# Low parts of weights and h in the first tile of the first MoE: from GpSimd to VectorE

## The chip, the cores and the metric

The kernel runs on one core of a Trainium2 chip. A core has TensorE (PE in the profile, its weight loads PEld), VectorE (DVE), ScalarE (ACT), GpSimd (POOL) and SyncE (SP, which here only issues transfers). The metric is the device time of one execution in microseconds.

## The reference, cut to what matters

Attention over chunks of 32 tokens gives x (3072 tokens, 512 wide). Two feed-forward blocks follow. The change lies in the first of them:

```python
def _moe_ref(x, w_gate, w_val, w_out, rms_g):      # w_gate, w_val 512 x 1536, w_out 1536 x 512
    rms = np.sqrt(np.mean(x * x, axis=-1, keepdims=True) + 1e-06)
    xn = x / rms * rms_g
    g = xn @ w_gate
    silu = g * (1.0 / (1.0 + np.exp(-g)))
    val = xn @ w_val
    return (silu * val @ w_out).astype(np.float32)
```

## The kernel before, in words

Every product of the feed-forward blocks is made of three matmuls: a float32 operand is split into a rounded **high part** and a **low part** (operand minus high part), and mm3 (L534 to L536) adds high x high, high x low and low x high. `split` makes the two parts: ScalarE writes the high part (L106), then an engine that the caller names writes the low part by one subtraction over 128 x 512 (L107).

The first MoE takes the tokens in tiles of 512; t counts the tiles, and this case is about t = 0. In a tile, f runs over 12 blocks of 128 hidden columns. For each f TensorE computes the gate product in ps_g0 and the value product in ps_g1 (12 matmuls each); ScalarE applies Silu (L811), VectorE multiplies (L816) to s, which is the h of this block, and `split_h` splits s into hh and hl. The output product of the block before (`out1`, 12 matmuls, which need hh and hl) follows on TensorE.

The weights come as 36 units in the order gate, value, out of f = 0, of f = 1 and so on. They arrive as float64 words, and in tile t = 0 one unit is converted at each of the 36 slots (three in each f):

- `load_w` transfers a unit into one of three buffers named w64 (L114, on SP's queue).
- `conv_c` scales one word half into a buffer tu (ScalarE, L122); there are three such buffers.
- `conv_d` joins the bits on VectorE, with three instructions in a chain (L132, L135, L138). When the last of them is done, the w64 buffer is free for the load of the unit three places on.
- `conv_g` splits tu into the high and low part in the resident tile `wall` (L106, L107). Then tu is free for the unit three places on.

The four units of the first slots are converted in a part written out by hand before the first tile (the string ORDER), and 32 are left for t = 0. Between the slots of t = 0 stand the steps of attention for later tokens, on TensorE with one PSUM tile ps_a: s (scores, L391; then VectorE takes m, L404, and e, L407, and ScalarE the exponential, L416), a (transpose of e, L421; ScalarE copies it to aT, L427), v (product with v, L437; VectorE normalizes, L458 to L464), r (row scaling on VectorE, L502) and x (transpose, L512; ScalarE copies it to xn, L523). One pair of such steps takes six values of f:

```python
plan = {1: "s0", 3: "a0", 4: "v0", 7: "s1", 9: "a1", 10: "v1", 11: "r0", 14: "x0", 15: "x1"}
```

In t = 0 only the queues of TensorE and SP are in the order in which the code is written; a scheduler sets the order on VectorE, ScalarE and GpSimd from its own estimate of the work. From t = 1 on every queue is in written order. All queues are executed strictly in order. Exponential and Silu need different tables on ScalarE, so each exponential brings two rows ACT_TABLE_LOAD.

Of the kernel before, what the change touches and what calls it, by code (L numbers as in the profile page):

```python
# [8 lines left out]
F32 = mybir.dt.float32  # L9
# [29 lines left out]
def tile_stream_attention_moe_moe2(  # L39
# [10 lines left out]
    nc = tc.nc  # L50
# [54 lines left out]
    def split(hi, lo, src, eng_lo):  # L105
        nc.scalar.activation(hi, src, AF.Copy)  # L106
        eng_lo.tensor_tensor(out=lo, in0=src, in1=hi.bitcast(F32), op=ALU.subtract)  # L107
# [9 lines left out]
    def conv_c():  # L117


        dst, key, w64 = raw.pop(0)  # L120
        tu = tmp.tile([P, 512], U32, tag="tu", name="tu")
        nc.scalar.activation(tu.bitcast(F32), words(w64)[1].bitcast(F32), AF.Copy, scale=2.0 ** -112)  # L122
        absd.append((dst, key, w64, tu))
# [18 lines left out]
    def conv_d():  # L142
        dst, key, w64, tu = absd.pop(0)
        join(tu, w64)
        f32s.append((dst, key, tu))

    def conv_g():
        dst, key, tu = f32s.pop(0)
        w = wall[:, 3 * key[1] + "gvo".index(key[0])]
        split(w[:, 0], w[:, 1], tu.bitcast(F32), nc.gpsimd)  # L150
        dst[key] = (w[:, 0], w[:, 1])

    def conv_w():

        n = len(absd)
        if f32s:
            conv_g()
        if raw:
            conv_c()
        if n:  # L160
            conv_d()
# [165 lines left out]
    def split_x(src):  # L327
        for kk in range(KK):
            x_hi(src, kk, slice(0, TT))
            x_lo(src, kk, slice(0, TT), nc.vector)  # L330
# [196 lines left out]
    def load_x(t):  # L527
        xn_t[t] = xs.tile([P, KK, TT], F32, tag="xn", name="xn")
        nc.sync.dma_start(xn_t[t], x_d[t])
# [8 lines left out]
    def proj_in(ps, unit):  # L538
        wh, wl = unit
        for kk in range(KK):  # L540
            sl = slice(kk * P, (kk + 1) * P)
            mm3(ps, (wh[:, sl], wl[:, sl]), xhl[kk], kk == 0, kk == KK - 1)

    h_t = {}

    def split_h(key, h, eng_lo):
        hi = hp_.tile([P, TT], F32R, tag="hh", name="hh")
        lo = hp_.tile([P, TT], F32R, tag="hl", name="hl")
        split(hi, lo, h, eng_lo)
        h_t[key] = (hi, lo)  # L550

    def evacuate(dst):
# [6 lines left out]
    def out1(t, f):  # L559
        h = h_t.pop(f)  # L560
        wh, wl = w1[("o", f)]
        for m in range(KK):
            sl = slice(m * P, (m + 1) * P)
            mm3(ps_y[m], (wh[:, sl], wl[:, sl]), h, f == 0, f == F1 - 1)
        if f == F1 - 1:
            ys = xs.tile([P, KK, TT], F32, tag="xn", name="ys")
            evacuate(ys)
            nc.sync.dma_start(y_d[t], ys)
# [26 lines left out]
    for st in ORDER.split():  # L595
# [28 lines left out]
        elif c == "r":  # L624
            step_r(n // 2, (n % 2,))
        elif c == "p":
            part_p(n)
        elif c in "HL":
            kk, o = divmod(n, 2)
            part = slice(o * PT, o * PT + PT)  # L630
            if c == "H":
                x_hi(xn_t[0], kk, part)
            else:
                x_lo(xn_t[0], kk, part, nc.gpsimd if st in LO_ON_POOL else nc.vector)
        elif c == "G":
            cols = slice(n % 2 * PT, n % 2 * PT + PT)
            for x in x_t[n // 2]:
                nc.gpsimd.tensor_tensor(out=x[:, cols], in0=x[:, cols], in1=g_b[:, cols], op=ALU.mult)
        elif c == "R":
            pr, blk = divmod(n, 2)  # L640
            x = x_t[pr][blk]
            nc.scalar.activation(x, x, AF.Copy, scale=rs_t[pr][:, blk:blk + 1])
        elif c == "c":
            conv_c()
        elif c == "d":
            conv_d()
            load_w(units1, 1)
        elif c == "g":
            conv_g()
        else:  # L650
            fns[c](n)
            if c in "mAn":
                free.append(use.pop(({"m": "s", "A": "a", "n": "v"}[c], n)))
# [56 lines left out]
    def slot(t, s):  # L710
        att_slot(t, s)
        if t == 0:
            conv_w()
            load_w(units1, 1)
        else:
            if xq:
                xq.pop(0)()

            n = 36 * t - 36 + s
            conv_step(2 if n < 48 else 7 / 3 if n < 88 else 3)  # L720
# [16 lines left out]
    def load_y(*src):  # L737
        for o in range(2):
            nc.sync.dma_start(m2["y"][:, o], src[o])


    def load_wp(n):
        if n < F1 + NP2 * G2:
            src = w1p_d[n] if n < F1 else w2p_d[(n - F1) % G2]
            nc.sync.dma_start(wp[:, n % 2].bitcast(F32), src)
# [17 lines left out]
    def x_steps(e):  # L763
        y = m2["y"]
        B11, B21, B12, B22 = y[:, 0, 0:2], y[:, 0, 2:4], y[:, 1, 0:2], y[:, 1, 2:4]
        tt = nc.vector.tensor_tensor

        def hi(c, x):
            nc.scalar.activation(xb[:, 2 * c:2 * c + 2, 0], x, AF.Copy)

        def lo(c, x):
            tt(
                out=xb[:, 2 * c:2 * c + 2, 1],
                in0=x,
                in1=xb[:, 2 * c:2 * c + 2, 0].bitcast(F32),
                op=ALU.subtract,
            )


        yield lambda: tt(out=e, in0=B12, in1=B11, op=ALU.subtract)  # L780
        yield lambda: tt(out=B12, in0=B22, in1=B12, op=ALU.subtract)
        yield lambda: (hi(0, B11), hi(2, e))
        yield lambda: (lo(0, B11), hi(3, B12))
        yield lambda: (tt(out=B11, in0=B12, in1=B11, op=ALU.add), hi(1, B11))
        yield lambda: (lo(1, B11), hi(4, B21))
        yield lambda: (lo(2, e), hi(5, B22))
        yield lambda: lo(3, B12)
        yield lambda: lo(4, B21)
        yield lambda: (tt(out=B21, in0=B21, in1=B11, op=ALU.subtract), hi(6, B21))
        yield lambda: lo(5, B22)  # L790
        yield lambda: lo(6, B21)

    for t in range(NS):
        if t == 1:
            region.close()
            region.enter_context(tc.manual_schedule())
        for f in range(F1):
            if t == NS - 1 and f == 6:
                att_only.close()
                right = ctx.enter_context(tc.tile_pool(name="right", bufs=1, side="right", reuse_waits="tile"))  # L800
                m2["y"] = right.tile([P, 2, KK, TT], F32, name="y")
                load_y(x_d[NS], x_d[NS + 1])
            if t == NS - 1 and f == 7:
                xq.extend(x_steps(xs.tile([P, 2, TT], F32, tag="xn", name="e")))
            if 0 < t < NS - 1 and f == 9:
                load_x(t + 1)
            if t == NS - 1 and f == F1 - 1:
                load_wp(0)
            proj_in(ps_g[0], w1[("g", f)])
            s = sp.tile([P, TT], F32, tag="s", name="s")  # L810
            nc.scalar.activation(s, ps_g[0], AF.Silu)  # L811
            slot(t, 3 * f)
            proj_in(ps_g[1], w1[("v", f)])
            if f == F1 - 1 and t + 1 < NS:
                split_x(xn_t.pop(t + 1))
            nc.vector.tensor_tensor(out=s, in0=s, in1=ps_g[1], op=ALU.mult)  # L816
            split_h(f, s, nc.gpsimd if t == 0 else nc.vector)
            slot(t, 3 * f + 1)
            if pend is not None:
                out1(*pend)  # L820
            pend = (t, f)
            slot(t, 3 * f + 2)
# [298 lines left out]
```

## Time and profile before

| | us |
|---|---|
| median of 3 runs | 1215.93 (1214.59 to 1216.49) |
| the profiled execution | 1213.37 |
| its span (first to last instruction) | 1211.6 |
| busy: TensorE matmul | 1169.8 (97%) |
| busy: VectorE | 761.2 (63%) |
| busy: ScalarE | 496.8 (41%) |
| busy: GpSimd | 171.2 (14%) |

The profiled execution is 1.8 us longer than its span. The busy shares are means over stages that differ; the tile t = 0 lies between about 41 and 168 us of the span.

### The profile page before, as it was taken

The numbers are of one execution on the slowest core, as the hardware profiler recorded it, in microseconds if no ns is written. First come the engines' busy times: TensorE is split into PE (matmuls) and PEld (weight loads), VectorE is DVE, ScalarE is ACT, GpSimd is POOL, SyncE is SP. The second block draws the span as 40 slices with busy tenths as digits, with TensorE's granted clock in tenths as the row PEclk, the third lists the DMA queues.
The fourth block names the chain that finished last, engine by engine and source line by source line (L and its number), as shares of the span: only waits on it lengthen the run. The fifth ranks groups of instructions, "written<-read, shape, count | busy, mean of one in ns | idle before, by whom it ended". The sixth has DMA issues, their size and how long they took to land.

```text
span 1211.6 us, 19907 instructions
## 1 busy us (share of the span) xinstructions
PE 1169.8 (97%) x7993; PEld 940.8 (78%) x7993; DVE 761.2 (63%) x1256; ACT 496.8 (41%) x830; POOL 171.2 (14%) x219
## 2 busy tenths in 40 slices
PE   7888899999999999889999999999999999999998
PEld 4666677777777778668888788888888888888887
DVE  5898856656656665866767728666176664466620
ACT  4665655455544653433333414334043332233310
POOL 2655421121221212212101000000000000000000
PEclk8898999999999999989999999999999999999999
DMA  8555538887957666489787766756565656555354
GB/s 300 181 187 179 185 113 276 289 287 252 327 178 232 208 230 219 177 319 322 284 355 267 291 226 237 266 195 243 198 223 197 260 199 219 198 209 191 131 191 156
DMA packets 98061, 278.60 MB, mean 230 GB/s; under 512 B 10032, under 2 KB 22320, under 8 KB 91568
## 3 DMA queue, kind: packets, MB, share of 16 engines
q1 hardware_dynamic: 79408, 218.59, 51.5%
q0 software_dynamic: 15104, 52.44, 12.1%
q10 hardware_dynamic: 3456, 6.29, 1.4%
q8 instruction: 63, 1.03, 0.3%
q14 instruction: 30, 0.25, 0.1%
HBM read 209.13 MB, written 68.16 MB: 229 GB/s over the span
## 4 chain that ended last, share of the span: by engine, by line
PE 54%; DMA 2%; DVE 2%; ACT 0%; issue 0%; POOL 0%; SPq 0%; DVEq 0%; ACTq 0%
PE ps_y L975 7%; PE ps_y L974 7%; PE ps_y L973 7%; PE ps_b L836 5%; PE ps_b L837 5%; PE ps_b L838 5%; PE ps_g L836 4%; PE ps_g L838 4%; PE ps_g L837 4%; PE ps_y L535 2%; PE ps_y L536 2%; PE ps_y L534 2%; DMA w<-in_w_dram 1%; DMA wo<-w1o_d 1%; DMA y_d<-ys 1%
## 5 line engine op out<-in xcount | busy, mean ns | idle before, releaser
L534 PE MATMUL ps_g<-xh,wall 128*128 128x512 f32 x384 | 159.3, 415 | 3.3 <-ACT s L811 2.2
L536 PE MATMUL ps_g<-xh,wall 128*128 128x512 f32 x384 | 153.6, 400 | 0.0
L535 PE MATMUL ps_g<-xl,wall 128*128 128x512 f32 x384 | 153.4, 400 | 0.0
L973 PE MATMUL ps_y<-wo,wall 128*128 128x512 f32 x324 | 126.0, 389 | 0.0
L974 PE MATMUL ps_y<-wo,wall 128*128 128x512 f32 x324 | 126.0, 389 | 0.0
L975 PE MATMUL ps_y<-wo,wall 128*128 128x512 f32 x324 | 126.0, 389 | 0.0
L897 ACT ACTIVATE t<-t,half 128x512 f32<-128x512 f32 x96 | 69.0, 720 | 132.0 <-DVE t L896 132.0
L836 PE MATMUL ps_b<-wall 128*128 128x512 f32 x288 | 112.8, 392 | 0.2 <-DVE p L869 0.2
L837 PE MATMUL ps_b<-wall 128*128 128x512 f32 x288 | 112.5, 391 | 0.0
L838 PE MATMUL ps_b<-wall 128*128 128x512 f32 x288 | 112.4, 390 | 0.0
L534 PEld LDWEIGHTS ps_g<-xh,wall 128*128 128x128 f32 x384 | 73.6, 192 | 21.9 <-ACT s L811 3.1
L836 PE MATMUL ps_g<-wall 128*128 128x512 f32 x216 | 84.5, 391 | 3.5 <-ACT p L863 3.5
L911 DVE TENSOR_TENSOR t<-t,ps_g 128x512 f32<-128x512 f32 x24 | 16.5, 688 | 112.6 <-PE ps_g L838 107.7
L536 PEld LDWEIGHTS ps_g<-xh,wall 128*128 128x128 f32 x384 | 73.2, 191 | 17.8
L535 PEld LDWEIGHTS ps_g<-xl,wall 128*128 128x128 f32 x384 | 73.7, 192 | 15.4
L838 PE MATMUL ps_g<-wall 128*128 128x512 f32 x216 | 84.3, 390 | 0.0
L837 PE MATMUL ps_g<-wall 128*128 128x512 f32 x216 | 84.3, 390 | 0.0
L534 PE MATMUL ps_y<-hh,wall 128*128 128x512 f32 x192 | 78.7, 410 | 1.0 <-ACT hh L106 1.0
L535 PE MATMUL ps_y<-hl,wall 128*128 128x512 f32 x192 | 75.9, 396 | 0.2 <-DVE hl L107 0.2
L536 PE MATMUL ps_y<-hh,wall 128*128 128x512 f32 x192 | 76.0, 396 | 0.0
L974 PEld LDWEIGHTS ps_y<-wo,wall 128*128 128x128 f32 x324 | 60.8, 188 | 12.7
L973 PEld LDWEIGHTS ps_y<-wo,wall 128*128 128x128 f32 x324 | 60.8, 188 | 12.6
(155 smaller groups left out, 2304.5 us busy)
## 6 DMA issues: line engine op xcount, KB each, us to landing
wo<-w2o_d SPq DMA_DIRECT2D x100, 512.0 KB, 4.7
wall<-w2p_d SPq DMA_DIRECT2D x24, 1792.0 KB, 7.4
wall<-w1p_d SPq DMA_DIRECT2D x12, 1792.0 KB, 8.8
w<-in_w_dram SPq DMA_DIRECT2D x36, 512.0 KB, 4.1
w<-in_w_dram POOLq DMA_DIRECT2D x32, 512.0 KB, 5.6
k_in<-in_k_dram SPq DMA_DIRECT2D x48, 256.0 KB, 4.4
wo<-w1o_d SPq DMA_DIRECT2D x24, 512.0 KB, 7.4
v_in<-in_v_dram SPq DMA_DIRECT2D x40, 260.0 KB, 4.1
```

Source lines behind the costliest of these rows:

```text
L534: nc.tensor.matmul(ps, wh, xh, start=start, stop=False)
L535: nc.tensor.matmul(ps, wh, xl, start=False, stop=False)
L536: nc.tensor.matmul(ps, wl, xh, start=False, stop=stop)
L836: nc.tensor.matmul(bank, wh, xh, start=st, stop=False, skip_group_check=True)
L837: nc.tensor.matmul(bank, wh, xl, start=False, stop=False, skip_group_check=True)
L838: nc.tensor.matmul(bank, wl, xh, start=False, stop=kk == 1, skip_group_check=True)
L897: nc.scalar.activation(s, s, AF.Square, scale=0.5, bias=half)
L911: tt(out=u2, in0=a, in1=b2, op=ALU.add)
L973: nc.tensor.matmul(ps_y[m], hi[:, sl], wh, start=b == 0, stop=False)
L974: nc.tensor.matmul(ps_y[m], hi[:, sl], wl, start=False, stop=False)
L975: nc.tensor.matmul(ps_y[m], lo[:, sl], wh, start=False, stop=b == F2 - 1)
```

## The change

In t = 0 the low parts of the weights (`conv_g` out of `conv_w`) and of h (`split_h`) are subtracted by VectorE. The calls out of ORDER keep GpSimd, and from t = 1 on h was split on VectorE before too.

```diff
-    def conv_g():
+    def conv_g(eng_lo=nc.gpsimd):
         dst, key, tu = f32s.pop(0)
         w = wall[:, 3 * key[1] + "gvo".index(key[0])]
-        split(w[:, 0], w[:, 1], tu.bitcast(F32), nc.gpsimd)
+        split(w[:, 0], w[:, 1], tu.bitcast(F32), eng_lo)
         dst[key] = (w[:, 0], w[:, 1])
     def conv_w():
         n = len(absd)
         if f32s:
-            conv_g()
+            conv_g(nc.vector)
...
-    def split_h(key, h, eng_lo):
+    def split_h(key, h):
         hi = hp_.tile([P, TT], F32R, tag="hh", name="hh")
         lo = hp_.tile([P, TT], F32R, tag="hl", name="hl")
-        split(hi, lo, h, eng_lo)
+        split(hi, lo, h, nc.vector)
         h_t[key] = (hi, lo)
...
-            split_h(f, s, nc.gpsimd if t == 0 else nc.vector)
+            split_h(f, s)
```

The orders of TensorE and SP are the same before and after. GpSimd loses 44 rows of L107 (32 of weights, 12 of h), and VectorE has them more; the scheduler also sets the other rows of VectorE and ScalarE anew. A number behind tu names a unit: tu_923 and tu_944 are the ninth and tenth of all, tu_967, tu_1036, tu_1057 and tu_1086 the next four.

**First place: VectorE around the first scores of the tile** (m_1023 and e_1025, from the step s in f = 2; s_963 is the h of f = 2). Before:

```order
L138 SCALAR_TENSOR_TENSOR tu_967<-w64_853,tu_967 128x512
L132 TENSOR_SCALAR tu_1036<-tu_1036 128x512
L135 SCALAR_TENSOR_TENSOR tu_1036<-w64_928,tu_1036 128x512
L138 SCALAR_TENSOR_TENSOR tu_1036<-w64_928,tu_1036 128x512
L132 TENSOR_SCALAR tu_1057<-tu_1057 128x512
L135 SCALAR_TENSOR_TENSOR tu_1057<-w64_949,tu_1057 128x512
L816 TENSOR_TENSOR s_963<-s_963,ps_g1_104 128x512
L138 SCALAR_TENSOR_TENSOR tu_1057<-w64_949,tu_1057 128x512
L404 TENSOR_REDUCE m_1023<-ps_a_102 128x8
L132 TENSOR_SCALAR tu_1086<-tu_1086 128x512
L407 TENSOR_TENSOR e_1025<-ps_a_102,m_1023 128x2x4x64
```

After:

```order
L138 SCALAR_TENSOR_TENSOR tu_967<-w64_853,tu_967 128x512
L816 TENSOR_TENSOR s_963<-s_963,ps_g1_104 128x512
L132 TENSOR_SCALAR tu_1036<-tu_1036 128x512
L135 SCALAR_TENSOR_TENSOR tu_1036<-w64_928,tu_1036 128x512
L404 TENSOR_REDUCE m_1023<-ps_a_102 128x8
L107 TENSOR_TENSOR hl_988<-s_963,hh_987 128x512
L407 TENSOR_TENSOR e_1025<-ps_a_102,m_1023 128x2x4x64
L107 TENSOR_TENSOR wall_97<-tu_967,wall_97 128x512
L138 SCALAR_TENSOR_TENSOR tu_1036<-w64_928,tu_1036 128x512
```

Between L138 of tu_967 and e stood nine rows and stand five: the end of tu_1036, all of tu_1057 and the start of tu_1086 went behind e, and one low part came ahead of it.

**Second place: ScalarE around its first copy to xn** (L523, in f = 4, which the transpose of step x in f = 5 waits for). Before:

```order
L106 ACTIVATE wall_97<-tu_1207 128x512
L122 ACTIVATE tu_1233<-w64_1166 128x512
L811 ACTIVATE s_1203<-ps_g0_103 128x512
L122 ACTIVATE tu_1260<-w64_1189 128x512
L106 ACTIVATE wall_97<-tu_1233 128x512
L122 ACTIVATE tu_1288<-w64_1212 128x512
L106 ACTIVATE wall_97<-tu_1260 128x512
L106 ACTIVATE hh_1227<-s_1203 128x512
L122 ACTIVATE tu_1314<-w64_1238 128x512
L106 ACTIVATE wall_97<-tu_1288 128x512
L523 ACTIVATE xn_1252<-ps_a_102 128x4x128
```

After:

```order
L811 ACTIVATE s_1203<-ps_g0_103 128x512
L122 ACTIVATE tu_1233<-w64_1166 128x512
L106 ACTIVATE wall_97<-tu_1184 128x512
L106 ACTIVATE wall_97<-tu_1207 128x512
L106 ACTIVATE hh_1227<-s_1203 128x512
L122 ACTIVATE tu_1260<-w64_1189 128x512
L523 ACTIVATE xn_1252<-ps_a_102 128x4x128
```

Three high parts (tu_1233, tu_1260, tu_1288), each behind its unit's L138 on VectorE, went behind the copy. On VectorE, after, the unit whose w64 buffer tu_1260 takes over is tu_1184, and its L138 stands here, behind the row scaling of step r:

```order
L502 SCALAR_TENSOR_TENSOR x_nat_905<-x_nat_905,rs_1153,g_b_99 128x512
L107 TENSOR_TENSOR wall_97<-tu_1161,wall_97 128x512
L135 SCALAR_TENSOR_TENSOR tu_1184<-w64_1062,tu_1184 128x512
L135 SCALAR_TENSOR_TENSOR tu_1207<-w64_1091,tu_1207 128x512
L138 SCALAR_TENSOR_TENSOR tu_1184<-w64_1062,tu_1184 128x512
L138 SCALAR_TENSOR_TENSOR tu_1207<-w64_1091,tu_1207 128x512
```

Two units are now joined side by side, where before one followed the other.

**Third place: ScalarE around the exponential of f = 7**, in the second half of the tile (e_1416). Before:

```order
L106 ACTIVATE wall_97<-tu_1477 128x512
L106 ACTIVATE hh_1378<-s_1354 128x512
L416 ACT_TABLE_LOAD
L416 ACTIVATE e_1416<-e_1416 128x512
L122 ACTIVATE tu_1552<-w64_1432 128x512
L811 ACT_TABLE_LOAD
L811 ACTIVATE s_1467<-ps_g0_103 128x512
L427 ACTIVATE aT_1473<-ps_a_102 128x512
```

After:

```order
L106 ACTIVATE hh_1378<-s_1354 128x512
L122 ACTIVATE tu_1448<-w64_1340 128x512
L122 ACTIVATE tu_1477<-w64_1363 128x512
L416 ACT_TABLE_LOAD
L416 ACTIVATE e_1416<-e_1416 128x512
L106 ACTIVATE wall_97<-tu_1427 128x512
L106 ACTIVATE wall_97<-tu_1448 128x512
L811 ACT_TABLE_LOAD
L811 ACTIVATE s_1467<-ps_g0_103 128x512
L427 ACTIVATE aT_1473<-ps_a_102 128x512
```

Two L122 moved ahead of the exponential, and two high parts stand between it and the table load that Silu and aT need.

## Rows read from the trace of the kernel before

**Rows 1.** Who waited for whom, 44 to 170 us; total, times, longest.

```profile
...
ACT wall L106 <- DVE tu L138: 42.3, 27, 3.4
...
PE ps_a L421 <- ACT e L416: 6.9, 2, 4.8
...
PE ps_a L512 <- ACT xn L523: 5.5, 1, 5.5
...
PE ps_a L437 <- ACT aT L427: 2.1, 2, 1.5
```

**Rows 2.** Stretches: length; PE, PEld, DVE, ACT, POOL busy; granted TensorE clock; DMA.

```profile
44.00:170.00 126.00, 111.59 (x956) 87.81 (x955) 104.27 (x139) 70.85 (x123) 63.97 (x46) 0.96 0.48 158
71.77:74.64 2.87, 2.87 (x9) 2.48 (x10) 1.58 (x3) 1.74 (x3) 1.05 (x1) 0.50 0.25 63
97.52:101.96 4.44, 4.44 (x13) 3.67 (x14) 4.37 (x5) 2.77 (x6) 2.46 (x2) 0.50 0.68 222
```

**Rows 3.** Line L107: durations in ns, minimum, median, maximum.

```profile
L107 POOL TENSOR_TENSOR wall<-tu,wall x36: 1282/1348/1736, 26.7 to 158.3; 128x512 fp32r<-128x512 f32 x36
L107 DVE TENSOR_TENSOR hl<-s,hh x36: 691/693/695, 174.8 to 525.6; 128x512 fp32r<-128x512 f32 x36
```

**Rows 4.** Groups of VectorE's instructions, 44 to 170 us; busy us, mean ns.

```profile
L138 DVE SCALAR_TENSOR_TENSOR tu<-w,tu 128x512 uint32<-128x512 uint32 x32 | 35.5, 1110 | 0.7
L135 DVE SCALAR_TENSOR_TENSOR tu<-w,tu 128x512 uint32<-128x512 uint32 x30 | 29.6, 987 | 0.7
L132 DVE TENSOR_SCALAR tu<-tu 128x512 uint32<-128x512 uint32 x30 | 20.4, 679 | 9.8 <-ACT tu L122 9.8
```

**Rows 5.** Lines L132 and L138 over the whole span, as in rows 3.

```profile
L132 DVE TENSOR_SCALAR tu<-tu x68: 371/421/1511, 14.6 to 673.9; 128x512 uint32<-128x512 uint32 x68
...
L138 DVE SCALAR_TENSOR_TENSOR tu<-w,tu x68: 674/692/1668, 15.8 to 675.0; 128x512 uint32<-128x512 uint32 x68
```

**Rows 6.** Timeline, 50.6 to 51.9 us: start, duration, engine, line.

```profile
51.05 1.46 POOL L107 TENSOR_TENSOR wall<-tu,wall 128x512 fp32r<-128x512 f32 x1 [1.29 <-ACT wall L106]
51.40 1.65 DVE L138 SCALAR_TENSOR_TENSOR tu<-w,tu 128x512 uint32<-128x512 uint32 x1
```

**Rows 7.** Timeline around the first scores' exponential; in brackets the idle time before.

```profile
61.88 1.67 DVE L138 SCALAR_TENSOR_TENSOR tu<-w,tu 128x512 uint32<-128x512 uint32 x1
...
70.37 0.68 DVE L407 TENSOR_TENSOR e<-ps_a,m 128x512 f32<-128x512 f32 x1
...
71.77 0.48 PE L421 MATMUL ps_a<-ident,e 128*128 128x128 f32 x1 [4.77 <-ACT e L416]
```

**Rows 8.** Timeline from step r to the first copy to xn.

```profile
85.06 2.43 DVE L502 SCALAR_TENSOR_TENSOR x_nat<-x_nat,rs,g_b 128x512 f32<-128x512 f32 x2 [0.80 <-POOL rs L496]
...
88.63 0.60 PE L512 MATMUL ps_a<-ident,x_nat 128*128 128x128 f32 x4
...
96.34 0.63 ACT L106 ACTIVATE wall<-tu 128x512 fp32r<-128x512 f32 x1 [2.50 <-DVE tu L138]
...
96.88 0.58 ACT L523 ACTIVATE xn<-ps_a 128x512 f32<-128x512 f32 x1
...
97.52 0.47 PE L512 MATMUL ps_a<-ident,x_nat 128*128 128x128 f32 x1 [5.48 <-ACT xn L523]
```

**Rows 9.** Timeline: an L138 and the L122 whose load waited for it.

```profile
60.02 0.69 DVE L138 SCALAR_TENSOR_TENSOR tu<-w,tu 128x512 uint32<-128x512 uint32 x1
...
65.11 0.68 ACT L122 ACTIVATE tu<-w 128x512 f32<-128x512 f32 x1 [0.90 <-DMA w<-in_w_dram]
```

**Rows 10.** Timeline: from a step a to its step v, 140 to 145 us.

```profile
140.81 0.66 PE L421 MATMUL ps_a<-ident,e 128*128 128x128 f32 x4 [2.10 <-ACT e L416]
...
142.41 1.28 ACT L811 ACT_TABLE_LOAD   x1
...
144.19 0.59 ACT L427 ACTIVATE aT<-ps_a 128x512 f32<-128x512 f32 x1
...
144.84 0.86 PE L437 MATMUL ps_a<-v_in,aT 64*32 64x65 f32 x64 [0.58 <-ACT aT L427]
```

## The prediction

> **What bounds the kernel now.** I read the page first: TensorE is busy almost throughout, so only a stretch in which it idles or runs slowly can give anything. The change touches the tile t = 0, about 41 to 168 us. There I read the waits: TensorE waits 6.9 us in two pieces for the exponential of e, 5.5 us in one piece for the copy to xn and 2.1 us in two pieces for aT, together 14.5 us [rows 1]. All are steps of attention; no wait for a low part is listed. Then the windows: behind the two long waits TensorE's granted clock is 0.50, the 1.2 GHz level, for 2.87 and 4.44 us [rows 2]. At the 2.4 GHz level the same work takes half of that, so these cost another 3.7 us. **The ceiling is 14.5 + 3.7 = 18.2 us.** Outside these waits TensorE runs on, and the change does nothing to its work.
>
> Who is late? ScalarE stands 42.3 us for L138 of VectorE [rows 1]; its exponential and copies are queued behind these high parts. VectorE is busy 104.3 of 126 us [rows 2], and many of its instructions are long: L138 has a mean of 1110 ns, L135 of 987 and L132 of 679 [rows 4], while the medians over the whole span are 692 for L138 and 421 for L132 [rows 5]. The timeline shows why: GpSimd's L107 starts at 51.05 and ends at 52.51; the L138 that starts at 51.40 ends at 53.05, 0.54 us behind GpSimd, after 1.65 us [rows 6]. Two-input instructions of VectorE stand still while GpSimd subtracts.
>
> **The change, part by part.** *Work on VectorE.* It takes 44 subtractions (32 for weights, 12 for h). One takes 691 ns there at least, against 1282 on GpSimd [rows 3]: 44 x 0.691 = 30.4 us more. With GpSimd silent, I let the three joining lines fall to their medians (L135 is of L138's form, so it gets the same 692): 32 x (1.110 - 0.692) = 13.4, 30 x (0.987 - 0.692) = 8.9, 30 x (0.679 - 0.421) = 7.7 [rows 4, 5], together 30.0 us less. The sum is +0.4 us: VectorE's work stays where it is, about 104.7 us. The bounds of the relief are 0 (the length has another cause) and 30.0; I take 30.0, since the rows lie beside each other in time. What GpSimd saves costs nothing and gives nothing else: the L198 and L199 transfers on its queue begin only after this tile.
>
> A rule speaks against the change: the Trainium skill, Perfetto Trace Analysis, section Optimizing Scalar/DVE Operations, says that work may be moved off a saturated VectorE, even to GpSimd; the change does the reverse on an engine that is 83% busy. Read so, the 30.4 us would come with no relief, which is the last rival below. The same section restricts it: the two share a read port, so that moving work between them may not help. This trace agrees with the restriction (1.65 us for 0.69, above).
>
> *The first long wait (4.8 us, and 1.4 at half clock).* Before, from the start of L138 of tu_967 (61.88) to the end of e (71.05) VectorE needs 9.2 us, and TensorE wants the exponential from 71.77 - 4.77 = 67.00 on [rows 7]. In the new order there stand L138, L816, L132, L135, m, hl and e: five of about 0.69, m and L816 being like e (0.68), one of 0.42, and hl at 0.69, in all 4.5 us. So e ends near 66.4 and its exponential (0.63, as a high part in [rows 8]) near 67.0. The wait goes. L132 of tu_1036 may come up to 0.8 us late, because its load can start only when an earlier L138 has freed the buffer; that is in the bounds below.
>
> *The second (5.5, and 2.2 at half clock).* Before, the copy at 96.88 follows a high part for which ScalarE had stood 2.50 us [rows 8], the last of three that now stand behind the copy. What is late next is a transfer: the copy stands behind L122 of tu_1260, whose load starts when L138 of tu_1184 is done. From the end of L502 to there: four instructions of 0.69, 2.8 us. From the end of an L138 to the L122 that waited for its load: 65.11 - 60.71 = 4.4 us [rows 9]. Then 0.68 and 0.58: xn is ready 8.5 us behind L502. TensorE does the first transpose and a gate product before it wants xn; a transpose and a product take 144.84 - 0.58 - 140.81 = 3.45 us [rows 10]. So it waits 8.5 - 3.45 = 5.0, less the time by which the transpose itself follows L502. That was 88.63 - 87.49 = 1.1 us [rows 8], so at most 3.9 remain; at the other end none, when VectorE gains on TensorE. I take the middle, **2.0 us**. The clock fell behind waits of 4.8 and 5.5 us; for one of 2.0 I count nothing.
>
> *The short waits.* The second exponential (2.1) and two aT (2.1) hang on ScalarE's own chain: a table load, Silu and aT are 144.78 - 142.41 = 2.37 us [rows 10], with high parts and L122 between, against TensorE's 3.45 us from a to v. The third place shows the chain no shorter. I keep **4.2 us**, between 0 and 5.5 (one table load of 1.28 more).
>
> *New ones.* Where the first e is no longer late, its own aT is next: before, the half clock hid it. I give it 1.0, the mean of the two aT that waited [rows 1]. In the third place two L122 come ahead of the exponential, 2 x 0.68 = 1.4, with no wait there before. Together **2.4 us**, between 0 and twice that.
>
> *Low parts for TensorE.* A weight's low part now queues on VectorE. L107 takes 0.69 instead of 1.35 us [rows 3] but stands behind others; the order puts it a slot or more ahead of its product. That costs nothing as long as VectorE keeps up, which is what the last rival disputes.
>
> **Sum.** 18.2 - (2.0 + 4.2 + 2.4) = 9.6 us gained; by the bounds between 18.2 - (3.9 + 5.5 + 4.8) = 4.0 and 18.2. The profiled execution took 1213.37, so it becomes 1203.8; the median of the runs lies 2.56 above the profiled one, so I forecast **1206.3 us**.
>
> **The rivals.** (1) *All waits go.* VectorE is so far ahead that neither copies nor exponentials come late: 16 to 18.2 us, about 1199 us. For it: the net work is zero and the order is better. Against it: 104.7 us of work in a stretch that would last 126 - 18.2 = 107.8 leaves VectorE 3 us of slack. (2) *The waits move and nothing is gained.* The loads (4.4 us each, three buffers) or ScalarE's chain set the pace again: 1216 us. For it: ScalarE stood 0.90 us for a load already [rows 9]; against it: with all waits gone the 36 slots take 126 - 18.2 = 107.8 us, 9.0 for three, and a loop of load, L122 and joining is 4.4 + 0.7 + 1.8 = 6.9 us for three units. (3) *VectorE becomes the bound, slower.* If the relief does not come, it has 104.3 + 30.4 = 134.7 us of work for a stretch of 126; TensorE then waits for low parts in `wall`, and the time is 8.7 us up: about 1224.6. It decides from a relief below 8.7 us on, even with VectorE never idle. Against it: [rows 6]. (4) That the change does not do what it says is excluded: the order shows no L107 left on GpSimd in this tile.
>
> **How the numbers follow.** A measurement of this kernel can tell about 0.2%, 2.4 us, from no change. The forecast as worked out (4.0 to 16 us gained) gets 0.64, rival 1 0.13, a rest of 2.4 to 4.0 us gained 0.05, rival 2 (within 2.4 us) 0.08, rival 3 0.10. So faster 0.82, same 0.08, slower 0.10. The range leaves out rivals 2 and 3 and the very end of rival 1: from 17.4 us gained, 1198.5, to 2.9 us gained, 1213.0.
>
> **What would show it.** Right: L138, L135 and L132 in the tile at 0.69 and 0.42 us; VectorE's busy time about the same; TensorE's wait for the first e gone, that for the first xn under 4 us; no granted clock of 0.50 between 45 us and the tile's end; everything from t = 1 on as before, about 10 us earlier. Wrong: joining lines that stay long with GpSimd idle (the relief), TensorE waiting for L107 of `wall` or hl (VectorE too late), or ScalarE standing for loads longer than the 4 us that I allow (the transfers pace the tile).

## The result

The change takes 1202.34 us (median of 4 runs, 1197.8 to 1203.44) against 1215.83 before (one run more than in the table above); the ratio is 0.9876, with a 95% interval of 0.9851 to 0.9902, some 12 to 18 us. The profiled execution took 1202.68 us with a span of 1200.9. The forecast of 1206.3 lay 4 us too high.

TensorE's waits in the tile t = 0 after the change, as in [rows 1] of before (total, times, longest):

```profile
PE ps_a L421 <- ACT e L416: 3.2, 2, 1.9
PE ps_g L536 <- DVE wall L107: 0.4, 1, 0.4
PE ps_a L512 <- ACT xn L523: 0.4, 1, 0.4
PE ps_a L437 <- ACT aT L427: 0.2, 1, 0.2
```

The 14.5 us are 4.2. One wait is of a new kind, 0.4 us for a low part of a weight. The windows, to be read beside [rows 2], show one stretch of the low clock where there were two:

```profile
44.00:160.00 116.00, 111.65 (x961) 87.62 (x960) 98.56 (x185) 72.68 (x125) 2.07 (x3) 0.99 0.53 174
...
129.02:132.50 3.48, 3.48 (x11) 2.89 (x12) 1.90 (x3) 3.45 (x6) 0.00 (x0) 0.51 0.57 160
```

At half clock (0.51) 3.48 us cost 1.7. What ScalarE stands for has changed too. Before, and then after:

```profile
ACT tu L122 <- DMA w<-in_w_dram: 3.2, 4, 1.9
```

```profile
ACT tu L122 <- DMA w<-in_w_dram: 18.3, 15, 2.9
...
ACT wall L106 <- DVE tu L138: 7.1, 10, 1.5
```

It stands 7.1 us for L138 of VectorE, 42.3 before, but 18.3 for loads of weights, 3.2 before.

The tile as a whole is measured from its first gate matmul to its last transpose of step x. Before:

```profile
38.75 0.85 PE L534 MATMUL ps_g<-xh,wall 128*128 128x512 f32 x1
...
160.16 0.60 PE L512 MATMUL ps_a<-ident,x_nat 128*128 128x128 f32 x4
```

After:

```profile
39.91 0.71 PE L534 MATMUL ps_g<-xh,wall 128*128 128x512 f32 x1
...
149.29 0.60 PE L512 MATMUL ps_a<-ident,x_nat 128*128 128x128 f32 x4
```

That is 121.4 us against 109.4, 12.0 less. Without waits and half clock both are about the same: 121.4 - 14.5 - 3.7 = 103.2 and 109.4 - 4.2 - 1.7 = 103.5. Behind the tile both need the same: 1211.6 - 160.16 = 1051.4 and 1200.9 - 149.29 = 1051.6. So, to within about 1 us, the gain is the waits that went. (In this execution the tile began 1.2 us later; what lies ahead of it has the same code. The start of the tile is at half clock in both, for 1.75 us before and 0.43 after; the sums leave this out.)

VectorE's groups in the tile, 44 to 160 us (busy us, mean ns), beside [rows 4]:

```profile
L135 DVE SCALAR_TENSOR_TENSOR tu<-w,tu 128x512 uint32<-128x512 uint32 x31 | 22.0, 719 | 0.2
L138 DVE SCALAR_TENSOR_TENSOR tu<-w,tu 128x512 uint32<-128x512 uint32 x32 | 21.6, 685 | 0.2
L107 DVE TENSOR_TENSOR wall<-tu,wall 128x512 fp32r<-128x512 f32 x32 | 21.6, 684 | 1.7 <-ACT wall L106 1.5
L132 DVE TENSOR_SCALAR tu<-tu 128x512 uint32<-128x512 uint32 x30 | 12.4, 422 | 5.2 <-ACT tu L122 5.0
L107 DVE TENSOR_TENSOR hl<-s,hh 128x512 fp32r<-128x512 f32 x12 | 8.3, 689 | 1.4 <-ACT hh L106 1.2
```

The joining lines have their short durations, and the two groups of L107 are the price, 29.9 us. Over the tile alone VectorE's busy time (DVE, columns as in [rows 2]) did not stay level, it fell. Before and after:

```profile
38.75:160.76 122.01, 107.60 (x875) 84.86 (x874) 106.21 (x140) 70.63 (x122) 65.07 (x48) 0.95 0.51 167
```

```profile
39.91:149.89 109.98, 105.63 (x875) 83.02 (x874) 97.81 (x183) 70.81 (x122) 4.00 (x5) 0.98 0.57 185
```

That is 8.4 us less. The durations of the rows add up to 112.9 and 110.1 us, 2.8 less, of which 2.0 are L502 (mean 1252 ns before, 748 after). The other 5.6 us are overlap: a row often starts a little before the row ahead of it ends (64.81 against 64.21 + 0.68 = 64.89, in the rows of the first long wait below), and after the change more rows do.

The hold-up itself can be read row by row in the trace of before. Of the 66 rows of L135 and L138 in the tile, 29 took more than 0.74 us, and each of them ended 0.55 us (0.545 to 0.553) behind a subtraction of GpSimd, as in [rows 6]. The 10 of 32 rows of L132 above 0.46 us each ended 0.28 us behind one. After the change 2 of the 66 are long, at the tile's start, where GpSimd's last subtractions stand.

### The profile page after: what moved, and what is told of

It is laid out like the page before. It is cut to its first block, busy times and chain, and to the rows that moved or that the text cites. A ratio compares the mean times of both kernels' runs of the same rounds, so it can differ in the third digit from the quotient of the medians.

```text
span 1200.9 us, 19871 instructions
## 1 busy us (share of the span) xinstructions
PE 1167.9 (97%) x7993; PEld 939.4 (78%) x7993; DVE 753.5 (63%) x1300; ACT 497.1 (41%) x830; POOL 108.1 (9%) x175
## 4 chain that ended last, share of the span: by engine, by line
PE 54%; DMA 2%; DVE 2%; ACT 0%; issue 0%; POOL 0%; DVEq 0%; ACTq 0%; SPq 0%
PE ps_y L973 7%; PE ps_y L975 7%; PE ps_y L974 7%; PE ps_b L836 5%; PE ps_b L838 5%; PE ps_b L837 5%; PE ps_g L836 4%; PE ps_g L837 4%; PE ps_g L838 4%; PE ps_y L535 2%; PE ps_y L536 2%; PE ps_y L534 2%; DMA w<-in_w_dram 1%; DMA y_d<-ys 1%; DMA wo<-w2o_d 1%
## 5 line engine op out<-in xcount | busy, mean ns | idle before, releaser
L836 PE MATMUL ps_b<-wall 128*128 128x512 f32 x288 | 112.9, 392 | 0.3 <-DVE p L869 0.2
L536 PEld LDWEIGHTS ps_g<-xh,wall 128*128 128x128 f32 x384 | 72.9, 190 | 18.3 <-DVE wall L107 0.8
```

The costliest lines, as they stand in the source:

```text
L536: nc.tensor.matmul(ps, wl, xh, start=False, stop=stop)
L836: nc.tensor.matmul(bank, wh, xh, start=st, stop=False, skip_group_check=True)
```

## The experiments

My theory: GpSimd's subtraction holds VectorE's two-input instructions up; moved over, the work on VectorE is level, and what is queued there comes earlier. Rivals: the scheduler's new order is the whole gain, or the length of VectorE's queue alone counts.

**One part alone.** In the first run h stays on GpSimd; in the second the weights do.

```diff
-            split_h(f, s)
+            split_h(f, s, nc.gpsimd if t == 0 else nc.vector)   # weights only
...
-            conv_g(nc.vector)
+            conv_g()                                             # h only
```

Weights only, 

> Only the 32 low parts of weights go to VectorE; the 12 of h stay on GpSimd, and the scheduler orders anew. Theory (GpSimd's subtractions hold VectorE's two-input instructions up, so that VectorE's total stays level and what is queued behind them comes earlier): 32 of 44 holders are gone, so some 32/44 of the 13.5 us gained remain, 10 us, about 1206, with L138 near 0.75 us in the tile. Rival (a long queue on VectorE is what counts, and each subtraction is simply added): the fewer subtractions go over the better, so faster than the whole change, below 1202.

Measured: 1208.03 us, ratio 0.994 (0.9924 to 0.9957), with L138 at 794 ns and L135 at 885.

h only, 

> Only the 12 low parts of h go to VectorE; the 32 of weights stay on GpSimd. Theory: 12/44 of the gain, 3 to 4 us, about 1212, and L138, L135 and L132 still long (means 0.9 to 1.1, 0.85 to 1.0 and 0.55 to 0.68 us). Rival (only the new place of the first scores in VectorE's queue counts, which the scheduler gives whenever hl stands on VectorE): the first long wait goes whole here too, so 6 us or more, below 1210.

Measured: 1215.66 us, ratio 1.0008 (0.9993 to 1.0023). VectorE's lines in both runs, 44 to 180 us, show how much of the hold-up each part leaves. Weights only:

```profile
L135 DVE SCALAR_TENSOR_TENSOR tu<-w,tu 128x512 uint32<-128x512 uint32 x31 | 27.3, 885 | 0.5
L138 DVE SCALAR_TENSOR_TENSOR tu<-w,tu 128x512 uint32<-128x512 uint32 x32 | 25.2, 794 | 0.3
```

h only, with TensorE's wait for exponentials:

```profile
PE ps_a L421 <- ACT e L416: 9.7, 3, 5.9
```

```profile
L138 DVE SCALAR_TENSOR_TENSOR tu<-w,tu 128x512 uint32<-128x512 uint32 x31 | 29.9, 965 | 0.6
L135 DVE SCALAR_TENSOR_TENSOR tu<-w,tu 128x512 uint32<-128x512 uint32 x30 | 29.2, 972 | 0.8
...
L107 DVE TENSOR_TENSOR hl<-s,hh 128x512 fp32r<-128x512 f32 x13 | 10.6, 813 | 2.2 <-ACT hh L106 2.1
```

For weights only the direction is as forecast and the gain short of it: 5 to 9 us by the interval, 10 expected. For h only the theory misses: 3 to 4 us were expected and none came. The new hl is itself held up (813 ns), and TensorE's longest wait for an exponential was still 5.9 us there. The rivals miss too. One part gives 7 us and the other 0, the whole change 13 to 15: they do not add up. The traces show that the subtractions left on GpSimd still find instructions to hold up: of the 66 rows of L135 and L138 in the tile, 11 end 0.55 us behind one for weights only and 21 for h only, against 29 before and 2 after the change. The scheduler set a new order in each run, too; how much of the missing gain is due to the order, these two runs do not show.

**The order taken out.** All queues of the tile in written order, with the low parts on either engine:

```diff
-    region.enter_context(tc.manual_schedule(engines={ET.PE, ET.SP}))
+    region.enter_context(tc.manual_schedule())
```

On VectorE, 

> The whole change, but in the first tile every queue is in the order in which the code is written, VectorE, ScalarE and GpSimd too, so the scheduler has no part in it. To be read against the next run, which has the same order and keeps the low parts on GpSimd. Theory: relief counts by itself, so this is at least 5 us faster than the next run. Rival (the scheduler's new order is the whole gain): the two are within 3 us of each other. Against the kernel before I expect 1200 to 1215.

Measured: 1235.24 us, ratio 1.0163 (1.0144 to 1.0181).

On GpSimd, 

> The kernel before with every queue of the first tile in written order; low parts on GpSimd. Theory: VectorE's joining lines are long as before (L138 about 1.1 us) and the time is at least 5 us above that of the run in written order with the low parts on VectorE; 1210 to 1235. Rival (order alone): within 3 us of it.

Measured: 1223.3 us, ratio 1.0065 (1.0046 to 1.0084). This went against the theory as it stood: with the low parts on VectorE the kernel is 12 us **slower**, though the relief is complete. Waits and groups of the run on VectorE, 44 to 180 us:

```profile
PE ps_g L534 <- ACT wall L106: 20.7, 10, 3.3
DVE wall L107 <- ACT wall L106: 20.0, 26, 1.7
DVE hl L107 <- ACT hh L106: 7.7, 11, 0.7
```

```profile
L135 DVE SCALAR_TENSOR_TENSOR tu<-w,tu 128x512 uint32<-128x512 uint32 x32 | 22.2, 692 | 1.1
L138 DVE SCALAR_TENSOR_TENSOR tu<-w,tu 128x512 uint32<-128x512 uint32 x32 | 22.1, 692 | 1.1
```

The run on GpSimd:

```profile
PE ps_g L536 <- POOL wall L107: 14.0, 11, 2.0
```

```profile
L138 DVE SCALAR_TENSOR_TENSOR tu<-w,tu 128x512 uint32<-128x512 uint32 x32 | 37.6, 1174 | 1.1
```

In written order a low part stands right behind its high part. GpSimd could stand there and wait (41.8 us for high parts of weights in the other run, at no cost to VectorE); VectorE cannot: it stood 27.7 us, with all its other work queued behind. In the other run L138 took 1174 ns and TensorE waited 14.0 us for low parts from GpSimd; against the kernel before it is 8.5 us slower, the price of the written order with the low parts left on GpSimd. The new theory: the change needs both, the relief and an order in which the low part comes well behind its high part, which the scheduler gave.

**The low part later.** The run on VectorE in written order, with one edit (hl is put behind the slot's conversions in the same way):

```diff
         if f32s:
-            conv_g(nc.vector)
+            dst, key, tu = f32s.pop(0)
+            w = wall[:, 3 * key[1] + "gvo".index(key[0])]
+            nc.scalar.activation(w[:, 0], tu.bitcast(F32), AF.Copy)
+            dst[key] = (w[:, 0], w[:, 1])
+            lo = (w, tu)
         if raw:
             conv_c()
         if n:
             conv_d()
+        if lo:
+            w, tu = lo
+            nc.vector.tensor_tensor(out=w[:, 1], in0=tu.bitcast(F32), in1=w[:, 0].bitcast(F32), op=ALU.subtract)
...
```

> The low parts on VectorE and all queues of the first tile in written order, as in the run that took 1235 us, with one edit: a low part is written behind the next unit's three joining lines, and hl behind that slot's conversions, so that VectorE does not stand for the high part it needs from ScalarE. There VectorE stood 20.0 us for high parts of weights and 7.7 us for hh. Theory (the gain of the change needs both, shorter lines and an order in which the low part comes later than its high part): these 27.7 us go, and the time falls by 18 to 30 us, to 1205 to 1217. Rival (written order is bad for another reason, such as TensorE waiting for high parts that ScalarE writes late): under 8 us, above 1227.

Measured: 1209.51 us, ratio 0.9936 (0.991 to 0.9962), 25.7 us less than the same order without the edit. Waits of the run, 44 to 170 us (L169 is the low part, L160 the high part, L546 the third matmul of mm3):

```profile
PE ps_g L546 <- DVE wall L169: 9.2, 7, 1.6
...
DVE wall L169 <- ACT wall L160: 1.6, 1, 1.6
...
DVE hl L561 <- ACT hh L559: 1.4, 2, 0.7
```

VectorE's 27.7 us are 3.0, and the time fell as the new theory said. What is left are 9.2 us of TensorE waiting for low parts that come a little late.

**The hold-up put back, the order kept.** The change, with an idle instruction on GpSimd beside each of the 32 conversions; the orders on VectorE and ScalarE are those of the change. The idle results are read by nobody.

```diff
+    def idle_pool(src):
+        nc.gpsimd.tensor_tensor(out=scrap[0], in0=src, in1=src, op=ALU.subtract)   # first run
+        nc.gpsimd.memset(scrap[0], 0.0)                                            # second run, in its place
...
         split(w[:, 0], w[:, 1], tu.bitcast(F32), eng_lo)
+        if eng_lo is nc.vector:
+            idle_pool(w[:, 0].bitcast(F32))
...
```

Subtractions, 

> The changed kernel, and beside each of the 32 conversions of the first tile a subtraction of a high part from itself on GpSimd, into a scrap tile that nobody reads; VectorE's and ScalarE's orders are those of the change, row by row. Theory (GpSimd's reading subtraction is what made VectorE's joining lines long): L138, L135 and L132 go back to means of 0.85 to 1.1, 0.85 to 1.0 and 0.45 to 0.7 us, VectorE gets 15 to 25 us more work with the same order, and the time goes up by 8 to 20 us, to 1210 to 1222. Rival (the new order is what counts, the length of these lines is not): within 3 us of the change, 1200 to 1205.

Measured: 1214.19 us, ratio 0.9982 (0.996 to 1.0003), so the gain is gone. The tile takes 120.2 us, measured as above (121.4 before, 109.4 with the change). Groups of VectorE's lines, 44 to 160 us (this file's lines lie a little lower: L137, L140 and L143 are the joining lines, L112 is the idle instruction):

```profile
L107 DVE TENSOR_TENSOR wall<-tu,wall 128x512 fp32r<-128x512 f32 x31 | 33.0, 1075 | 0.1
L140 DVE SCALAR_TENSOR_TENSOR tu<-w,tu 128x512 uint32<-128x512 uint32 x31 | 25.7, 836 | 0.2
L143 DVE SCALAR_TENSOR_TENSOR tu<-w,tu 128x512 uint32<-128x512 uint32 x31 | 21.5, 704 | 0.2
L137 DVE TENSOR_SCALAR tu<-tu 128x512 uint32<-128x512 uint32 x30 | 14.1, 479 | 3.9 <-ACT tu L127 3.9
```

The time came as expected, and the hold-up too, but on other lines: it is mostly L107 that is held up, and L143 hardly is. (L107 and the idle subtraction wait for the same high part.) One of the pairs, and the tile as a whole:

```profile
52.55 1.15 POOL L112 TENSOR_TENSOR scrap<-wall 128x512 f32<-128x512 f32 x1 [3.76 <-ACT wall L106]
52.72 1.53 DVE L107 TENSOR_TENSOR wall<-tu,wall 128x512 fp32r<-128x512 f32 x1
```

```profile
38.66:159.45 120.79, 109.29 (x876) 83.87 (x874) 114.75 (x183) 71.09 (x123) 48.84 (x36) 0.96 0.52 169
```

GpSimd's row ends at 53.70 and VectorE's at 54.25, again 0.55 us later. VectorE is busy 114.7 us in the tile, against 97.8 with the change, for the same 183 rows. So a hold-up of 17 us on VectorE, at one order, takes the whole gain away. What the relief would give at the order of before, no run shows.

Constants, 

> As the run with idle subtractions, but GpSimd writes a constant into the scrap tile (128 x 512) 32 times and reads nothing. If it is GpSimd's reading that holds VectorE up, the joining lines stay at 0.69 and 0.42 us and the time is that of the change, 1200 to 1205. If any work of GpSimd on SBUF does, they are long as with the subtractions and the time is 1208 or more.

Measured: 1206.14 us, ratio 0.9906 (0.9882 to 0.993), just above the 1200 to 1205 expected; its interval overlaps that of the change. The 32 writes ran close together at the tile's start, from 40.5 to 62.8 us. VectorE's timeline beside them:

```profile
50.30 0.69 DVE L137 TENSOR_SCALAR tu<-tu 128x512 uint32<-128x512 uint32 x1
51.02 0.69 DVE L140 SCALAR_TENSOR_TENSOR tu<-w,tu 128x512 uint32<-128x512 uint32 x1
51.75 0.69 DVE L143 SCALAR_TENSOR_TENSOR tu<-w,tu 128x512 uint32<-128x512 uint32 x1
```

The two-input lines keep their 0.69 us; the one-input line takes 0.69 instead of 0.42. Since the writes did not lie beside the whole tile, the time says little; the rows say that an instruction of GpSimd that only writes does not hold the two-input lines, and so that its reading does.

**A lead for the conversions.** The run with the late low part, with the conversions one or two slots ahead, and the change once more:

```diff
+    for _ in range(1):      # 2 in the second run
+        conv_w()
+        load_w(units1, 1)
     pend = None
```

One slot, 

> The run in written order with late low parts, and the conversions of the first tile one slot ahead of TensorE (one more call of the conversion step and one load before the tile). There TensorE waited 9.2 us in 7 pieces for low parts of weights. Theory (with the joining lines short VectorE keeps pace with TensorE, and what is left is lead): half or more of these 9.2 us go, 1201 to 1206. Rival (VectorE has no time to spare, so that a lead is used up at once): within 2 us of the run without the lead, 1207 to 1212.

Measured: 1203.55 us, ratio 0.9898 (0.9874 to 0.9922); TensorE waited 1.6 us for low parts instead of 9.2. The waits went as expected; the interval of the ratio still touches that of the run without the lead.

Two slots, 

> The same with two slots of lead. Theory: nearly all of the 9.2 us go, and the time is that of the change or below, 1198 to 1203. Rival: no better than with one slot, or worse, because the first f now waits for the conversions that stand ahead of it on VectorE: 1205 to 1212.

Measured: 1205.0 us, ratio 0.9899 (0.9876 to 0.9922); no wait for low parts, but 5.9 us for aT, xn and an exponential. So the theory's 1198 to 1203 did not come; two slots are no better than one, as the rival had it.

The change, 

> The change itself once more, on the same chip as the two runs with a lead: a ratio between 0.985 and 0.991 to the kernel before, 1198 to 1206, and waits in its first tile within 2 us of those of the first profile (TensorE 3.2 us for exponentials, at most one stretch at half clock).

Measured: 1203.18 us, ratio 0.9893 (0.9868 to 0.9918); TensorE waited 1.9 us for exponentials and 0.7 us for the rest, with no half clock behind them. A lead takes the waits for low parts away, and the written order ends where the scheduler's does, not below it: none of the versions tried beats the change.

## Why the prediction was right

**What bounds the kernel.** Right: the tile without waits and half clock is 103.2 and 103.5 us, so nothing but the 18.2 us of the ceiling was to be had.

**Work on VectorE, +30.4 and -30.0.** Measured: 32 x 0.684 + 12 x 0.689 = 30.2 more, and with the means of before and after 32 x 0.425 + 30 x 0.268 + 30 x 0.257 = 29.4 less. That two rows lay beside each other in time was no proof. The 29 long rows that all end 0.55 us behind a subtraction are, and the idle subtractions show what it is worth: they bring a hold-up back at one order, and the gain goes. Wrong is the sum in another way: "VectorE's busy time about the same" was to be a sign, and it fell by 8.4 us in the tile. L502 is held up no longer, which the sum left out, and the overlap of rows it did not have. So VectorE had more slack than the 3 us that the prediction held against the first rival.

**The first long wait.** Right. The exponential starts at 65.53, and TensorE takes it up without a wait:

```profile
64.21 0.68 DVE L107 TENSOR_TENSOR hl<-s,hh 128x512 fp32r<-128x512 f32 x1
64.81 0.68 DVE L407 TENSOR_TENSOR e<-ps_a,m 128x512 f32<-128x512 f32 x1
...
65.53 0.64 ACT L416 ACTIVATE e<-e 128x512 f32<-128x512 f32 x1
...
67.40 0.60 PE L421 MATMUL ps_a<-ident,e 128*128 128x128 f32 x4
```

**The second, 2.0 us.** Mis-sized: 0.4. The mechanism is as forecast; the copy stands behind an L122 whose load is late:

```profile
79.65 0.74 DVE L502 SCALAR_TENSOR_TENSOR x_nat<-x_nat,rs,g_b 128x512 f32<-128x512 f32 x1
...
82.81 0.60 PE L512 MATMUL ps_a<-ident,x_nat 128*128 128x128 f32 x4
...
86.41 0.67 ACT L122 ACTIVATE tu<-w 128x512 f32<-128x512 f32 x1 [1.75 <-DMA w<-in_w_dram]
86.98 0.58 ACT L523 ACTIVATE xn<-ps_a 128x512 f32<-128x512 f32 x1
...
87.61 0.66 PE L512 MATMUL ps_a<-ident,x_nat 128*128 128x128 f32 x4 [0.36 <-ACT xn L523]
```

From L502 to the end of the copy it is 87.56 - 80.39 = 7.2 us, not 8.5, mostly because the load came 3.6 us behind its L138 and not 4.4; the transpose follows L502 by 2.4 us, not 1.1; and transpose and product took 4.4 us (82.81 to 87.25), not 3.45, mostly since TensorE stood in them for a high part (0.3 us) and a low part (0.4) of a weight.

**The short and the new waits, 4.2 + 2.4.** Mis-sized: 3.2 us for the two exponentials (3.5 in the forecast), 0.2 for aT (3.1 in the forecast). The aT, not the exponentials, made this term too large. The second exponential has the forecast size (1.86 us, 2.1 forecast), but not for the reason given. Before, it stood for VectorE; after, the L122 ahead of its table load stands for a load, and TensorE stands for the exponential. Before:

```profile
140.13 0.63 ACT L416 ACTIVATE e<-e 128x512 f32<-128x512 f32 x1 [0.70 <-DVE e L407]
```

After:

```profile
126.35 0.67 ACT L122 ACTIVATE tu<-w 128x512 f32<-128x512 f32 x1 [2.92 <-DMA w<-in_w_dram]
...
129.02 1.09 PE L421 MATMUL ps_a<-ident,e 128*128 128x128 f32 x4 [1.86 <-ACT e L416]
```

So the size is luck here: neither was ScalarE's own chain alone. On the other side stand two terms that I had at nothing: 0.4 us for a low part, and 1.7 us at half clock behind this wait of 1.86 us; the sign "no granted clock of 0.50" failed there. So 5.9 us were left where I had 8.6, and the tile gained 12.0 instead of 9.6. That the forecast came within 4 us owes something to luck: 4.8 us of waits too many and 2.1 us too few partly cancel.

**What the prediction left unsaid.** I took the level sum on VectorE as the ground of the gain. The written orders show that it is not enough: with the full relief and the low part in the wrong place the kernel is 20 us slower than before (8.5 of them come with the written order on GpSimd already). Rival 3 had the right sign for that case and the wrong mechanism: VectorE was not short of time, it stood and waited for ScalarE.

## What to carry to other kernels

A subtraction on a second engine is no free help when it slows the first one by as much as it takes off it; look for long and short durations of one instruction and for what ran beside the long ones, and see whether the long ones all end at one distance behind it. When the work goes to the busy engine, put it behind other work of that engine, far from the instruction that it waits for: an idle engine may wait in its queue, a full one may not. Parts of such a change need not add up, so half of it can be worth nothing.

## What the runs showed of the hardware

GpSimd writing constants left VectorE's two-input lines at 0.69 us and took the one-input shift L132 from 0.42 to between 0.54 and 0.83 us; GpSimd subtracting lengthened both. A held-up row ended 0.55 us (two inputs) or 0.28 us (L132) behind the end of the GpSimd row that held it, whatever the length of that row. The Trainium skill, SBUF — State Buffer, section Who interferes with whom, says that an instruction of VectorE with two inputs in SBUF contends with a GpSimd instruction that reads SBUF, not with one that only writes it, and that one-input work contends in its two-port modes. The rows agree on the two-input lines; that L132 ran in such a mode, no run here shows by itself.

The clock did not follow the length of the wait alone: behind a wait of 1.86 us it stood at 0.51 for 3.48 us in one execution of the change, while behind one of 2.10 us before (at 140.81) it stayed at 1.00 in the windows that follow.
